# A fused attention, MLP and gated-convolution kernel: forty-eight VectorE operations moved to other engines, more buffers in the last stage, new planner numbers, issue in emission order

## The chip, the cores and the metric

The kernel runs on one core of one Trainium2 chip. The metric is the device time in microseconds (us) of one execution. The engines are PE (TensorE; PEld is its weight load), DVE (VectorE), ACT (ScalarE), POOL (GpSimd) and SP (SyncE, which here only issues DMAs).

## The reference

Three stages in a row, on 4 batches of 768 positions and 384 = 8 x 48 features, all in fp32:

```python
f = 1.0 / (1.0 + np.exp(-f_logit))
for t in range(S):                                   # gated linear attention, 8 heads of 48
    state = f[:, :, t, :, None] * state + np.einsum('bhd,bhe->bhde', k[:, :, t], v[:, :, t])
    y[:, :, t] = np.einsum('bhd,bhde->bhe', q[:, :, t], state)
...
xn = (x - mu) / np.sqrt(var + 1e-06) * g_ln          # layer norm, MLP 384 -> 1536 -> 384
ch = np.maximum(xn @ w_ch1, 0.0) @ w_ch2
x = x + ch
...
h = np.maximum(x @ w_in, 0.0)                        # 384 -> 1024, 3-tap convolution, gate
gate = 1.0 / (1.0 + np.exp(-conv_out))               # conv_out: 3 taps along the sequence
return (h * gate @ w_out).astype(np.float32)
```

## The kernel before, in words

The sequence is cut into 24 chunks `t` of 128 positions (6 per batch) and 8 units `u` of three chunks.

- `chunk(t)` is the attention of a chunk and the layer norm behind it. DVE scans the forget gate (`e`, L471) and its clipped inverse (`w`, L473), multiplies q by `e` (`qe`, L477), k by `w` (`kw`, L479), corrects that by one Newton step (L481, L483: the corrected k is what the scores wait for), and masks the scores (`am`, L502). Then come the sum `x` (ACT), its statistics (L640, L641), the reciprocal deviation `rs` on POOL (L645, L649), the normalized `xn` (DVE, L653), its fp16 high part (ACT) and low part (`xl`, DVE, L657), and a DMA transpose into `xnT`.
- `first(u)` and `second(u, tt)` are the MLP in pairs of fp16 numbers, three matmuls for each product. "c1" is its first half (L675 to L677), done chunk by chunk for the first two units and a unit at a time (384 columns) from the third on. "c2" is its second half (L744 to L746); behind it DVE adds the residual (`x2`, L756) and splits the sum (L761), and a DMA transposes it into `x2T`.
- `gate(u)` is the gated convolution: matmuls "h2" (L795 to L797), relu into `hr`, three taps into `cv` (L812, L817), the gate (L827, L832), and matmuls "o" (L846 to L848), then `ob` (ACT) and the output DMA.
- Weights arrive as raw 64-bit words; DVE decodes them (L374, L377, L380) and splits them (L421) in the first 140 us, between the work of the chunks.

What sets the order is `Plan`: each piece of work is a job with an engine, an assumed duration, a due time (`key`), what it depends on and which buffers it takes. `Plan.run` plays the jobs through in assumed time and emits their instructions in that order; the framework's own scheduler then reorders them once more for each engine. Due times come from a period `CP` per chunk and offsets (`T0`, `C1`, `C2`, `H2`, `O`, `EV`, `W1`, `W2`, `WI`). Each engine runs its instructions strictly in the order that results. All ACT instructions carry the line of the helper `act` (L316); they are told apart by tiles. Buffers: `hr`, `cv` two each, `ob` one, `x` five.

Of the kernel before, what the change touches and what calls it, by code (L numbers as in the profile page):

```python
# [20 lines left out]
DM = H * D  # L21
# [9 lines left out]
UT = 3  # L31
# [24 lines left out]
KV_DMA = 12  # L56
SW = CH + 1


CP = 22.8  # L60
T0 = 32.5
ATT = 0.3
C1 = 64.0
C2 = 21.0
H2 = 8.0
O = 39.0
EV = 29.0
# [8 lines left out]
def decode(nc, dst, tmp, raw):  # L76
    hi = raw[:, :, 1]
    nc.vector.tensor_scalar(
        out=tmp, in0=hi, scalar1=3, scalar2=0x3FFFFFFF,
        op0=ALU.logical_shift_left, op1=ALU.bitwise_and,  # L80
    )
    nc.vector.scalar_tensor_tensor(
        out=tmp, in0=hi, scalar=-0x40000000, in1=tmp, op0=ALU.bitwise_and, op1=ALU.bitwise_or
    )
    nc.vector.scalar_tensor_tensor(
        out=dst.bitcast(U32), in0=raw.bitcast(U32)[:, :, 0], scalar=29, in1=tmp.bitcast(U32),
        op0=ALU.logical_shift_right, op1=ALU.bitwise_or,
    )

# [24 lines left out]
class Plan:  # L114
# [7 lines left out]
    LAT = {"PE": 0.25, "DVE": 0.1, "ACT": 0.1, "POOL": 0.15, "SP": 2.5, None: 0.0}  # L122
# [37 lines left out]
    def run(self):  # L160
# [6 lines left out]
        while todo:  # L167
# [19 lines left out]
            free[e] = t + j.dur  # L187
            end = t + j.dur + j.lat
# [17 lines left out]
def fast_path(  # L206
# [20 lines left out]
    nc.vector.memset(fbs[0], 20.0)  # L227
# [6 lines left out]
    make_identity(nc, ident)  # L234
    d1 = const.tile([128, NP, SW], BF16, name="d1")
# [11 lines left out]
    nc.gpsimd.memset(fbs[1], 20.0)  # L247
# [32 lines left out]
    bufs("rs", 2, [128, 1], F32)  # L280
    bufs("xs", 2, [128, 2, DM], F16)
# [106 lines left out]
    def prep1(m, key):  # L388
# [10 lines left out]
        for z, kcs in enumerate(((0, 1), (2,))):  # L399
# [9 lines left out]
            j = P.job("PE", 0.55 * len(kcs), key, mm, [d, *his, J["diag"]], [bank], [use])  # L409
# [17 lines left out]
    def load_chunk(t):  # L427
        b, c = divmod(t, NCH)
        key = due_att(t) - 30.0

        def ldf():
            for j in range(2):
                nc.sync.dma_start(out=P("fb", t)[64 * j:64 * j + D, :, 1:], in_=f_[b, c, j])

        def ldqk():
            for j in range(2):
                nc.sync.dma_start(out=P("qk", t)[64 * j:64 * j + D], in_=qk_[b, c, j])

        def ldv():
            nc.sync.dma_start(out=P("vv", t), in_=v[b, c * CH:(c + 1) * CH, :])  # L440
        J["f", t] = transfer(0.9, key, ldf, ("fb", t), DM * CH * 4)
        J["qk", t] = transfer(0.9, key + 2.0, ldqk, ("qk", t), 2 * DM * CH * 4)
        J["v", t] = transfer(0.45, key + 4.0, ldv, ("vv", t), DM * CH * 4)

    def chunk(t):
# [19 lines left out]

        a1 = act(N, key + 1, e, fb, AF.Tanh, [J["f", t]], [E_], [F_], scale=0.5)
# [10 lines left out]
        qe = dv(N, 6, lambda: nc.vector.tensor_tensor(out=q_(), in0=q_(), in1=e3(), op=ALU.mult),  # L477
                [s1, J["qk", t]], (), [E_, Q_])
        kw = dv(N, 7, lambda: nc.vector.tensor_tensor(out=k_(), in0=k_(), in1=w3(), op=ALU.mult),  # L479
                [s2, J["qk", t]], (), [W_, Q_])  # L480
# [20 lines left out]
        sc = P.job("PE", 0.9, key + 10, scores, [kn, qe], [("sc", t)], [Q_])  # L501
# [15 lines left out]
        if not last and not dma:  # L517
# [15 lines left out]
            if c == 0:  # L533
# [6 lines left out]
                J["state", t] = P.job("DVE", 0.55, key + 14, upd, [kv], SN, [KV, E_])  # L540
            else:
# [10 lines left out]
                J["state", t] = P.job("DVE", 0.55, key + 14, upd, [j], SN, [K_, E_])  # L552
        elif not last:
# [10 lines left out]
                out=kT(), in_=ks().rearrange("p a b c -> p (a b c)")), [kl], [T_], [S_], lat=3.0)  # L564
# [8 lines left out]
            kv = P.job("PE", 0.65, key + 15, keyvals, [kT_, vl], [KV], [T_, ("vs", t)])  # L573
            if c == 0:
# [3 lines left out]
                J["state", t] = P.job("ACT", 0.5, key + 16, upd, [kv], SN, [KV])  # L578
            else:
# [11 lines left out]
                J["state", t] = P.job("DVE", 0.55, key + 16, upd, [j, kv], SN, [K_, KV])  # L591
# [3 lines left out]
        if c > 0:  # L595
# [6 lines left out]
            pre = [P.job("PE", 0.9, key + 16, inter, [qe, am, *old], [Y], [Q_, *SO])]  # L602
# [11 lines left out]
        else:  # L614
# [16 lines left out]
            ya = P.job("PE", 0.75, key + 17, intra, [al, vl, *pre], () if pre else [Y],  # L631
# [11 lines left out]
        def rstd():  # L643
# [6 lines left out]
        bn = P.job("DVE", 0.6, key + 19, stats, [xc], [ST], [X_])  # L650
        rs = P.job("POOL", 1.0, key + 20, rstd, [bn], [RS], [ST])
        N_, XS = ("xn", t), ("xs", t)
        xn = dv(DM, 21, lambda: nc.vector.tensor_scalar(  # L653
            out=P(*N_), in0=x(), scalar1=mv[:, 0:1], scalar2=P(*RS), op0=ALU.subtract,
            op1=ALU.mult), [rs], [N_], [X_, RS], V2)
        xh = act(DM, key + 22, lambda: P(*XS)[:, 0], lambda: P(*N_), AF.Copy, [xn], [XS], [N_])
        xl = dv(DM, 23, lambda: nc.vector.tensor_tensor(  # L657
            out=P(*XS)[:, 1], in0=P(*N_), in1=P(*XS)[:, 0], op=ALU.subtract), [xh], (), [N_, XS])
# [5 lines left out]
            [xl], () if tt else [XT], [XS] + ([XT] if tt else []), lat=3.0)  # L664
# [68 lines left out]
    def second(u, tt, started):  # L733
# [3 lines left out]
        bank = ("B", f"c2.{t}")  # L737
        o = lambda: P(*bank)[:, :DM]
        j = None
        for m0 in range(0, M1, 3):  # L740
            def mm(m0=m0):
                for m in range(m0, m0 + 3):
                    h = P(f"h{m}.{tt}", u)
                    nc.tensor.matmul(o(), h[:, 0], w2s[:, 0, m, :], start=(m == 0), stop=False)  # L744
# [4 lines left out]
                "PE", 1.47, key + 0.5 * m0, mm,  # L749
                [*(J["h", u, m, tt] for m in ms), *(z for m in ms for z in J["w2", m // 2]),  # L750
                 *([j] if j else started)],
                () if m0 else [bank], [(f"h{m}.{tt}", u) for m in ms] + ([bank] if m0 else []),
# [3 lines left out]
        x2 = P.job("DVE", V(DM), key, lambda: nc.vector.scalar_tensor_tensor(  # L756
            out=P(*X2), in0=o(), scalar=2.0 ** -9, in1=P("x", t), op0=ALU.mult, op1=ALU.add),
            [j], [X2], [bank, ("x", t)])
        h = act(DM, key, lambda: P(*XS)[:, 0], lambda: P(*X2), AF.Copy, [x2], [XS], [X2], scale=4.0)
        norm2(lambda: P(*X2), DM, X2_MAX ** -0.5, acc_col(), key + 1.0, [x2], [X2])  # L760
        lo = P.job("DVE", V(DM), key, lambda: nc.vector.scalar_tensor_tensor(  # L761
            out=P(*XS)[:, 1], in0=P(*X2), scalar=4.0, in1=P(*XS)[:, 0], op0=ALU.mult,
# [6 lines left out]
            lat=3.0)  # L769


    def gate(u):
# [9 lines left out]
        for m in range(M2):  # L782
# [38 lines left out]
            tp = P.job("DVE", 1.06, key, taps, [a], (), [HR, CV])  # L821
# [13 lines left out]
        for tt in range(UT):  # L835
# [18 lines left out]
            OB = ("ob", t)  # L854
# [53 lines left out]
    for u in range(NU):  # L908
        gate(u)
    for i, w_ in enumerate((w1s, w2s, wis, wos)):  # L910
# [5 lines left out]
    P.run()  # L916
# [270 lines left out]
```

## Time and profile before

| what | value |
|---|---|
| median of 3 runs (lowest, highest) | 645.26 us (643.96, 645.92) |
| the profiled execution: its own time / its span | 643.46 us / 641.4 us |
| busy PE, DVE, ACT, POOL | 586.1, 501.0, 386.2, 42.1 us (91, 78, 60, 7% of the span) |

The span runs from the first to the last instruction; 2.1 us of the profiled execution's own time lie outside it. Busy times are sums over the whole run: the early stretch, the middle and the end have different limits, so the shares say little until they are read stretch by stretch. On PE and DVE one instruction's shown duration reaches into the next one's, so that the distance between two starts is what an instruction costs in a queue without gaps.

### The profile page before, as it was taken

What the parts mean: (1) busy time and instruction counts of PE and PEld (TensorE: products, weight loads), DVE (VectorE), ACT (ScalarE), POOL (GpSimd) and SP (SyncE); (2) the same over time, 40 slices, a digit from 0 to 9 for tenths busy, and PEclk for the clock granted to TensorE, in tenths of its full rate; (3) what the DMA queues carried; (4) which work ended last, traced back from release to release, by engine and by line L of the source; (5) the groups of instructions that cost most, each with busy time, mean ns of one, the idle gap of its engine ahead of it and who ended that gap; (6) DMA issues with size and microseconds to landing.
All of it is one profiled execution on the core that took longest, in us unless ns stands there. A gap on an engine that the chain in (4) does not pass through costs nothing.

```text
span 641.4 us, 11836 instructions
## 1 busy us (share of the span) xinstructions
PE 586.1 (91%) x4680; PEld 392.7 (61%) x4680; DVE 501.0 (78%) x801; ACT 386.2 (60%) x798; POOL 42.1 (7%) x102
## 2 busy tenths in 40 slices
PE   1869898999798999999989999999989999999993
PEld 1758586767465666666656666666646666665551
DVE  6999989999999898976898787787895773326681
ACT  5888767779896575643675573554563662316471
POOL 3010110010101100010001000010000000000000
PEclk9979999999979899999989999999989999999998
DMA  8757567623224212541521203433221002001001
GB/s 255 184 168 186 175 141 181 189 55 75 68 58 123 63 41 48 143 77 28 103 54 54 80 20 75 118 78 58 46 42 50 14 13 51 25 1 38 25 13 42
DMA packets 75262, 52.24 MB, mean 81 GB/s; under 512 B 51904, under 2 KB 67264, under 8 KB 75200
## 3 DMA queue, kind: packets, MB, share of 16 engines
q1 hardware_dynamic: 75200, 51.42, 31.9%
q8 instruction: 38, 0.62, 0.4%
q14 instruction: 24, 0.20, 0.1%
HBM read 34.63 MB, written 4.72 MB: 61 GB/s over the span
## 4 chain that ended last, share of the span: by engine, by line
PE 53%; DVE 27%; ACT 8%; DMA 4%; issue 4%; POOL 2%; SPq 0%; DVEq 0%; ACTq 0%
PE B L675 5%; PE B L676 5%; PE B L677 5%; PE B L744 5%; PE B L746 5%; PE B L745 5%; PE B L848 4%; PE B L846 4%; PE B L847 4%; PE B L795 2%; PE B L796 2%; PE B L797 2%; DVE tw L377 2%; DVE cv L812 2%; DVE cv L827 2%
## 5 line engine op out<-in xcount | busy, mean ns | idle before, releaser
L675 PE MATMUL B<-xnT,w1s 128*128 128x128 f16 (+1 forms) x432 | 109.2, 275 | 3.0 <-DMA xnT<-xs 3.0
L677 PE MATMUL B<-xnT,w1s 128*128 128x128 f16 (+1 forms) x432 | 109.0, 275 | 0.3 <-ACT w1s L316 0.3
L676 PE MATMUL B<-xnT,w1s 128*128 128x128 f16 (+1 forms) x432 | 109.2, 275 | 0.0
L744 PE MATMUL B<-w2s,hh 128*128 128x384 f16 x288 | 94.5, 329 | 3.1 <-ACT w2s L316 2.1
L746 PE MATMUL B<-w2s,hh 128*128 128x384 f16 x288 | 94.7, 329 | 1.0 <-DVE hh L681 1.0
L745 PE MATMUL B<-w2s,hh 128*128 128x384 f16 x288 | 94.7, 329 | 0.9 <-DVE w2s L421 0.7
L681 DVE SCALAR_TENSOR_TENSOR hh<-B,hh 128x384 f16<-128x384 f32 (+1 forms) x90 | 51.4, 578 | 35.5 <-ACT hh L316 35.1
L795 PE MATMUL B<-x2T,wis 128*128 128x385 f16 x192 | 64.0, 334 | 5.9 <-ACT hr L316 5.9
L846 PE MATMUL B<-wos,g 128*128 128x384 f16 x192 | 63.7, 332 | 3.6 <-ACT g L316 3.6
L848 PE MATMUL B<-wos,g 128*128 128x384 f16 x192 | 63.3, 331 | 2.5 <-DVE g L832 2.4
L796 PE MATMUL B<-x2T,wis 128*128 128x385 f16 x192 | 64.1, 334 | 0.0
L797 PE MATMUL B<-x2T,wis 128*128 128x385 f16 x192 | 64.1, 334 | 0.0
L316 ACT ACTIVATE hh<-B 128x384 f16<-128x384 f32 (+1 forms) x90 | 44.5, 504 | 32.2 <-PE B L677 32.0
L847 PE MATMUL B<-wos,g 128*128 128x384 f16 x192 | 63.4, 330 | 0.0
L676 PEld LDWEIGHTS <-w1s 128*128 128x128 f16 x432 | 42.6, 99 | 16.8 <-issue 4.2
L675 PEld LDWEIGHTS <-w1s 128*128 128x128 f16 x432 | 43.3, 100 | 14.0 <-issue 0.7
L677 PEld LDWEIGHTS <-w1s 128*128 128x128 f16 x432 | 42.6, 99 | 14.9 <-issue 0.5
L812 DVE SCALAR_TENSOR_TENSOR cv<-hr,cws,cv 128x383 f32<-128x383 f32 (+1 forms) x64 | 38.8, 611 | 14.3 <-ACT cv L316 13.8
L497 PE MATMUL sc__144<-qk 64*128 64x128 f32 x384 | 29.6, 292 | 13.9 <-DVE qk L483 13.9
L746 PEld LDWEIGHTS <-hh 128*128 128x128 f16 x288 | 28.3, 98 | 21.8 <-issue 2.1
L744 PEld LDWEIGHTS <-hh 128*128 128x128 f16 x288 | 28.8, 100 | 20.6 <-issue 2.4
L316 ACT ACTIVATE cv<-hr,cws 128x384 f32<-128x384 f32 x64 | 38.7, 610 | 2.5 <-DVE g L832 1.3
(154 smaller groups left out, 1208.8 us busy)
## 6 DMA issues: line engine op xcount, KB each, us to landing
qk<-in_qk__dram SPq DMA_DIRECT2D x48, 192.0 KB, 3.5
raw<-in_w_dram SPq DMA_DIRECT2D x12, 768.0 KB, 5.4
vv<-in_v_dram SPq DMA_DIRECT2D x24, 192.0 KB, 2.5
fb<-in_f__dram SPq DMA_DIRECT2D x48, 96.0 KB, 2.7
out_dram<-ob SPq DMA_DIRECT2D x24, 192.0 KB, 1.9
raw<-in_wi_dram SPq DMA_DIRECT2D x6, 512.0 KB, 4.1
raw<-in_wo_dram SPq DMA_DIRECT2D x4, 768.0 KB, 4.3
xnT<-xs SPq DMA_TRANSPOSE x24, 2.5
```

Source lines behind the costliest of these rows:

```text
L316: nc.scalar.activation(out=out(), in_=in_(), func=func, **{a: z() if callable(z) else z for a, z in kw.items()},)
L675: nc.tensor.matmul(o, w1s[:, 0, kc, ms], x0, start=(kc == 0), stop=False)
L676: nc.tensor.matmul(o, w1s[:, 0, kc, ms], x1, start=False, stop=False)
L677: nc.tensor.matmul(o, w1s[:, 1, kc, ms], x0, start=False, stop=(kc == KC - 1))
L744: nc.tensor.matmul(o(), h[:, 0], w2s[:, 0, m, :], start=(m == 0), stop=False)
L745: nc.tensor.matmul(o(), h[:, 0], w2s[:, 1, m, :], start=False, stop=False)
L746: nc.tensor.matmul(o(), h[:, 1], w2s[:, 0, m, :], start=False, stop=(m == M1 - 1))
L796: nc.tensor.matmul(o, wis[:, 0, kc, ms], r1, start=False, stop=False)
L797: nc.tensor.matmul(o, wis[:, 1, kc, ms], r0, start=False, stop=(kc == KC - 1))
L846: nc.tensor.matmul(p, g[:, 0, ts_], wos[:, 0, m, :], start=(m == 0), stop=False)
L847: nc.tensor.matmul(p, g[:, 0, ts_], wos[:, 1, m, :], start=False, stop=False)
L848: nc.tensor.matmul(p, g[:, 1, ts_], wos[:, 0, m, :], start=False, stop=(m == M2 - 1))
```

## The change

- Chunks 0 to 9 (k: 1 to 9): the products `qe` and `kw` and the low part `xl` are computed by POOL. For these chunks ACT computes `xn` and its high part from `x` with a scale and a bias (a new POOL instruction makes the bias `mb`), in two independent passes.
- Chunks 0 to 8: the residual is added by PE: c2 begins with an fp32 matmul of `x` with a scaled identity (`ident2`), and ACT and DVE read the sum from PSUM. L756 goes for these chunks.
- The last stage gets more buffers: when the last two chunks are done with them, the two `qk` tiles become two more `hr`, and `am` and `as` two more `cv`; the output tiles of the last two units are taken from the five `x` tiles in place of the one `ob`.
- f is laid out by the host so that 128 partitions are filled by one DMA (before: two of 48 partitions each).
- The planner's assumed durations, latencies and due times have new numbers (one line of each kind is shown below), and `Plan.run` is called inside `tc.manual_schedule()`: what it emits is what each engine issues, in that order.

```diff
+POOL_Q = range(0, 10)
+POOL_K = range(1, 10)
+POOL_X = range(0, 10)
+XN_ACT = range(0, 10)
+X2_PE = range(0, 9)
+OBX = 2
...
-CP = 22.8
+CP = 22.6
...
-H2 = 8.0
+H2 = -23.6
...
+            if e == "POOL":
+                free["DVE"] += 0.2 * max(0.0, j.dur - 0.8)
...
+    G = lambda n: 0.15 + n * 2.2e-3
...
-            for j in range(2):
-                nc.sync.dma_start(out=P("fb", t)[64 * j:64 * j + D, :, 1:], in_=f_[b, c, j])
+            nc.sync.dma_start(out=P("fb", t)[:, :, 1:], in_=f_[b, c])
...
+        def tt(n, dk, fn, deps, takes=(), uses=(), pool=True):
+
+            if pool:
+                return P.job("POOL", G(n), key + dk, lambda: fn(nc.gpsimd), deps, takes, uses)
+            return dv(n, dk, lambda: fn(nc.vector), deps, takes, uses)
...
+        qe = tt(N, 6, lambda v_: v_.tensor_tensor(out=q_(), in0=q_(), in1=e3(), op=ALU.mult),
+                [s1, J["qk", t]], (), [E_, Q_], t in POOL_Q)
+        kw = tt(N, 7, lambda v_: v_.tensor_tensor(out=k_(), in0=k_(), in1=w3(), op=ALU.mult),
+                [s2, J["qk", t]], (), [W_, Q_], t in POOL_K)
...
+            scaled = lambda o, dk, deps, takes, uses: act(
+                DM, key + dk, o, x, AF.Identity, deps, takes, [*uses, X_, RS, MB],
+                scale=lambda: P(*RS), bias=lambda: P(*MB))
+            xn = scaled(lambda: P(*N_), 21, [mb], [N_], [])
+            xh = scaled(lambda: P(*XS)[:, 0], 22, [mb], [XS], [])
...
+        xl = tt(DM, 23, lambda v_: v_.tensor_tensor(
+            out=P(*XS)[:, 1], in0=P(*N_), in1=P(*XS)[:, 0], op=ALU.subtract), [xh], (), [N_, XS],
+            t in POOL_X)
...
+                if m0 == 0 and pe:
+                    nc.tensor.matmul(o(), ident2, P("x", t), start=True, stop=False)
...
+        if pe:
+            X2, x2, x2s_, two = bank, j, o, 2.0 ** -9
...
-            OB = ("ob", t)
+            OB = ("x", f"o{t}") if u >= NU - OBX else ("ob", t)
...
+    def more():
+
+        for name, a, shape in (
+            *(("hr", flat3(z), HT + 8) for z in qks),
+            ("cv", flat(P.pools["am"].tiles[0]), HT),
+            ("cv", flat3(P.pools["as"].tiles[0]).bitcast(F32), HT),
+        ):
...
-    P.run()
+    with tc.manual_schedule():
+        P.run()
```

How the queues move is shown at three places. First DVE at chunk 6, from its scan of `e` on, before the change; `tw`, `w__` and `wos` belong to the decoding of weights, `hh` to the MLP:

```order
L471 SCALAR_TENSOR_TENSOR e_111<-e_111,d_83 128x516
L756 SCALAR_TENSOR_TENSOR x_0_140<-B_148,x_127 128x384
L374 TENSOR_SCALAR tw_154<-raw_152 128x768
L477 TENSOR_TENSOR qk_70<-qk_70,e_111 128x512
L421 SCALAR_TENSOR_TENSOR wos<-w__0_155,wos 128x768
L761 SCALAR_TENSOR_TENSOR x2s_141<-x_0_140,x2s_141 128x384
L377 SCALAR_TENSOR_TENSOR tw_154<-raw_152,tw_154 128x768
L681 SCALAR_TENSOR_TENSOR hh_137<-B_150,hh_137 128x4x128
L380 SCALAR_TENSOR_TENSOR w__1_156<-raw_152,tw_154 128x768
L473 SCALAR_TENSOR_TENSOR w_113<-w_113,d_84 128x516
L502 SCALAR_TENSOR_TENSOR am_121<-sc__144,mask 128x1024
```

The same place of DVE's queue with the change (L499 is the scan of `e`, L501 that of `w`, L509 the Newton product, L811 the split behind c2):

```order
L499 SCALAR_TENSOR_TENSOR e_114<-e_114,d_85 128x516
L403 SCALAR_TENSOR_TENSOR w__1_160<-raw_157,tw_158 128x512
L397 TENSOR_SCALAR tw_158<-raw_155 128x768
L501 SCALAR_TENSOR_TENSOR w_115<-w_115,d_86 128x516
L444 SCALAR_TENSOR_TENSOR wis<-w__1_160,wis 128x512
L400 SCALAR_TENSOR_TENSOR tw_158<-raw_155,tw_158 128x768
L509 TENSOR_TENSOR w_115<-w_115,e_114 128x4x128
L403 SCALAR_TENSOR_TENSOR w__0_159<-raw_155,tw_158 128x768
L668 BN_STATS st_132<-x_126 128x6
L669 BN_AGGR mvs<-st_132 128x2
L811 SCALAR_TENSOR_TENSOR x2s_145<-B_149,x2s_145 128x384
```

The two products with q and k, the `x2` sum and `xn` are gone from the queue; the Newton product stands three rows behind the scan of `w` and now waits for POOL's product.

Second, POOL's queue around one chunk of the early stretch, before:

```order
L475 COPY pall<-e_111 128x4
L645 TENSOR_SCALAR rs_132<-mvs 128x1
L649 TENSOR_TENSOR rs_132<-rs_132,mhalf 128x1
L475 COPY pall<-e_112 128x4
L645 TENSOR_SCALAR rs_131<-mvs 128x1
L649 TENSOR_TENSOR rs_131<-rs_131,mhalf 128x1
```

and with the change:

```order
L505 TENSOR_TENSOR qk_71<-qk_71,e_114 128x512
L503 COPY pall<-e_114 128x4
L507 TENSOR_TENSOR qk_71<-qk_71,w_115 128x512
L673 TENSOR_SCALAR rs_133<-mvs 128x1
L677 TENSOR_TENSOR rs_133<-rs_133,mhalf 128x1
L683 TENSOR_SCALAR mb_135<-mvs,rs_133 128x1
L697 TENSOR_TENSOR xs_137<-xn_125,xs_137 128x384
```

Three products of 512 or 384 columns and the bias have come in; `rs` of one chunk now stands behind the products of another.

Third, PE at the first c2, with the change (before, L744 follows L677 there with nothing between):

```order
L718 MATMUL B_154<-xnT_139,w1s 128x128
L636 MATMUL B_150<-vv_116,am_123 128x48 x8
L785 MATMUL B_153<-x_126,ident_83 128x384
L788 LDWEIGHTS hh_141
L788 MATMUL B_153<-w2s,hh_141 128x384
```

The fp32 matmul L785 with the scaled identity (`ident2`, whose number the row leaves out) opens the accumulation of c2 in the same bank.

## Rows read from the trace of the kernel before

**Rows 1.** The page, 40 equal slices: busy tenths, granted TensorE clock in tenths.

```profile
PE   1869898999798999999989999999989999999993
PEclk9979999999979899999989999999989999999998
```

**Rows 2.** Stretches: us, each engine's busy us (instructions), PEclk, DMA share, GB/s.

```profile
0.00:16.00 16.00, 2.72 (x20) 2.50 (x21) 10.63 (x15) 8.17 (x19) 5.67 (x31) 1.00 0.85 255
16.00:219.00 203.00, 178.07 (x1709) 135.98 (x1708) 191.21 (x301) 160.14 (x355) 19.17 (x33) 0.95 0.50 130
...
320.00:360.00 40.00, 37.13 (x283) 23.59 (x282) 33.93 (x54) 24.06 (x45) 3.38 (x6) 0.96 0.23 62
...
440.00:480.00 40.00, 37.02 (x299) 23.91 (x298) 33.80 (x59) 23.67 (x48) 2.25 (x5) 0.96 0.30 53
480.00:595.00 115.00, 115.00 (x772) 70.92 (x769) 58.48 (x98) 50.08 (x96) 1.47 (x4) 1.00 0.10 27
595.00:633.00 38.00, 35.21 (x212) 19.96 (x210) 23.69 (x38) 20.74 (x35) 0.00 (x0) 1.00 0.06 21
```

**Rows 3.** Waits of PE, 13 to 219 us: total, times, longest.

```profile
PE sc__144 L497 <- DVE qk L483: 13.9, 3, 13.3
```

**Rows 4.** Waits of PE, 219 to 595 us.

```profile
PE B L795 <- ACT hr L316: 5.9, 2, 3.0
```

**Rows 5.** The end in order of time: last matmul of "o", last output copies.

```profile
631.96 0.33 PE L848 MATMUL B<-wos,g 128*128 128x384 f16 x1
...
634.35 0.49 ACT L316 ACTIVATE ob<-B 128x384 f32<-128x384 f32 x1 [1.99 <-DMA out_dram<-ob]
```

**Rows 6.** DVE in order of time at 120 us: start, duration in us.

```profile
119.71 0.56 DVE L756 SCALAR_TENSOR_TENSOR x<-B,x 128x384 f32<-128x384 f32 x1
120.18 0.55 DVE L374 TENSOR_SCALAR tw<-raw 128x768 int32<-128x768 int32 x1
120.65 0.68 DVE L477 TENSOR_TENSOR qk<-qk,e 128x512 f32<-128x512 f32 x1
121.25 0.95 DVE L421 SCALAR_TENSOR_TENSOR wos<-w__0_155,wos 128x768 f16<-128x768 f32 x1
```

**Rows 7.** Groups by line: shapes, count, busy us, mean ns of one, idle before.

```profile
L477 DVE TENSOR_TENSOR qk<-qk,e 128x512 f32<-128x512 f32 x24 | 16.4, 683 | 0.1
L756 DVE SCALAR_TENSOR_TENSOR x<-B,x 128x384 f32<-128x384 f32 x24 | 13.2, 551 | 23.4 <-PE B L746 23.2
...
L316 ACT ACTIVATE xs<-xn 128x384 f16<-128x384 f32 x24 | 12.5, 522 | 28.2 <-DVE xn L653 28.1
L653 DVE TENSOR_SCALAR xn<-x,mvs,rs 128x384 f32<-128x384 f32 x24 | 11.5, 479 | 15.2 <-POOL rs L649 15.2
```

**Rows 8.** The `x2` instructions of L756 alone, by stretches: us, DVE busy (instructions).

```profile
0.00:219.00 219.00, 3.31 (x6) 0.95 0.53 139
```

**Rows 9.** Waits of DVE, 16 to 219 us.

```profile
DVE xn L653 <- POOL rs L649: 5.8, 10, 0.7
```

**Rows 10.** POOL by shape: count, busy us, mean ns of one.

```profile
L248 POOL MEMSET qk<- 128x1024 f32 x1 | 1.0, 955 | 0.0
...
L924 POOL MEMSET one<- 128x1 f32 x1 | 0.1, 93 | 0.0
```

**Rows 11.** POOL's copy beside a DVE scan, and beside the masking that reads PSUM.

```profile
8.29 1.21 DVE L473 TENSOR_TENSOR_SCAN w<-w,d 128x516 f32<-128x516 f32 x1
...
8.43 1.04 POOL L475 COPY pall<-e 128x4 f32<-128x4 f32 x1 [3.58 <-DVE e L471]
...
17.73 1.20 DVE L502 SCALAR_TENSOR_TENSOR am<-sc__144,mask 128x1024 f32<-128x1024 f32 x1
17.87 0.19 POOL L475 COPY pall<-e 128x4 f32<-128x4 f32 x1 [7.97 <-DVE e L471]
```

**Rows 12.** PE in order of time at 22 us: an fp32 matmul of 256 columns.

```profile
22.29 0.60 PE L407 MATMUL B<-w__1_156,diag 128*128 128x256 f32 x2
22.72 0.27 PE L408 MATMUL B<-w1s,nident 128*128 128x256 f16 x1
```

More of the change, by code (lines that the diff above doesn't have):

```diff
@@ L121 @@
     ENGINES = ("PE", "DVE", "ACT", "POOL", "SP", "DMA", None)
-    LAT = {"PE": 0.25, "DVE": 0.1, "ACT": 0.1, "POOL": 0.15, "SP": 2.5, None: 0.0}
+    LAT = {"PE": 0.2, "DVE": 0.13, "ACT": 0.13, "POOL": 0.15, "SP": 2.5, None: 0.0}
     def __init__(self):
@@ L539, in upd @@
                         )
-                J["state", t] = P.job("DVE", 0.55, key + 14, upd, [kv], SN, [KV, E_])
+                J["state", t] = P.job("DVE", 0.75, key + 14, upd, [kv], SN, [KV, E_])
             else:
@@ L551, in upd @@
                         )
-                J["state", t] = P.job("DVE", 0.55, key + 14, upd, [j], SN, [K_, E_])
+                J["state", t] = P.job("DVE", 0.75, key + 14, upd, [j], SN, [K_, E_])
         elif not last:
@@ L590, in upd @@
                         )
-                J["state", t] = P.job("DVE", 0.55, key + 16, upd, [j, kv], SN, [K_, KV])
+                J["state", t] = P.job("DVE", 0.75, key + 16, upd, [j, kv], SN, [K_, KV])
         Y = ("B", f"y{t}")
@@ L741, in mm @@
             def mm(m0=m0):
+                if m0 == 0 and pe:
+                    nc.tensor.matmul(o(), ident2, P("x", t), start=True, stop=False)
                 for m in range(m0, m0 + 3):
                     h = P(f"h{m}.{tt}", u)
-                    nc.tensor.matmul(o(), h[:, 0], w2s[:, 0, m, :], start=(m == 0), stop=False)
+                    nc.tensor.matmul(
+                        o(), h[:, 0], w2s[:, 0, m, :], start=(m == 0 and not pe), stop=False)
                     nc.tensor.matmul(o(), h[:, 0], w2s[:, 1, m, :], start=False, stop=False)
@@ L748, in second @@
             j = P.job(
-                "PE", 1.47, key + 0.5 * m0, mm,
+                "PE", 1.47 + (0.66 if pe and not m0 else 0.0), key + 0.5 * m0, mm,
                 [*(J["h", u, m, tt] for m in ms), *(z for m in ms for z in J["w2", m // 2]),
                  *([j] if j else started)],
-                () if m0 else [bank], [(f"h{m}.{tt}", u) for m in ms] + ([bank] if m0 else []),
+                () if m0 else [bank],
+                [(f"h{m}.{tt}", u) for m in ms] + ([bank] if m0 else [("x", t)] if pe else []),
             )
@@ L755, in second @@
         X2, XS = ("x2", t), ("x2s", t)
[L756 to L760, printed above, removed]
+        if pe:
+            X2, x2, x2s_, two = bank, j, o, 2.0 ** -9
+        else:
+            x2s_, two = lambda: P(*X2), 1.0
+            x2 = P.job("DVE", V(DM), key, lambda: nc.vector.scalar_tensor_tensor(
+                out=P(*X2), in0=o(), scalar=2.0 ** -9, in1=P("x", t), op0=ALU.mult, op1=ALU.add),
+                [j], [X2], [bank, ("x", t)])
+        h = act(DM, key, lambda: P(*XS)[:, 0], x2s_, AF.Copy, [x2], [XS], [X2], scale=4.0 * two)
+        norm2(x2s_, DM, two * X2_MAX ** -0.5, acc_col(), key + 1.0, [x2], [X2])
         lo = P.job("DVE", V(DM), key, lambda: nc.vector.scalar_tensor_tensor(
[L762 removed]
+            out=P(*XS)[:, 1], in0=x2s_(), scalar=4.0 * two, in1=P(*XS)[:, 0], op0=ALU.mult,
             op1=ALU.subtract), [h], (), [X2, XS])
@@ L909, in fast_path @@
         gate(u)
+    def more():
[4 more added lines that the diff above has]
+        ):
+            s = P.pools[name]
+            s.free.append((mj.ready, len(s.tiles)))
+            s.tiles.append(a[:, :2 * shape].rearrange("p (a c) -> p a c", a=2))
+    mj = P.job(None, 0.0, 0.0, more, [J["late"], *(
+        j for j in P.jobs if any(
+            p in ("qk", "am", "as") and k in (NT - 2, NT - 1) for p, k in (*j.takes, *j.uses)))])
     for i, w_ in enumerate((w1s, w2s, wis, wos)):
```

91 lines of the change are left out of this document (52 added, 39 removed).

## The prediction

> **What bounds the kernel now.** I read the run by stretches, since the limits differ. The slices show PE nearly full from about 220 us to 600 us and full of holes before [rows 1]. [...] So three cases follow each other: a start of 13.3 us in which PE waits for the first corrected k [rows 3]; an early stretch to 219 us which DVE sets; and a PE-bound rest. In the rest only two holes of some 3 us show, in 320 to 360 and 440 to 480 us [rows 2], where PE waits for a relu on ACT to free a bank [rows 4]. At the end the last matmul starts at 631.96 us, but the last output copy only at 634.35 us, because it waited 1.99 us for the previous output DMA to free the one `ob` [rows 5].
>
> What the early stretch can give is bounded by PE: 203 - 178.07 = 24.9 us of idle time, and 203 x 0.05 = 10 us for the clock, 35 us together. Time saved on DVE later than 219 us is worth little.
>
> **What DVE loses in work.** An instruction of DVE costs the distance between starts: 120.18 - 119.71 = 0.47 us for one of 384 columns and 121.25 - 120.65 = 0.60 us for one of 512 [rows 6], each 0.08 us less than its mean duration of 551 or 683 ns; for `xn` that gives 479 - 80 = 0.40 us [rows 7]. Up to 219 us these go: ten `qe`, 6.0; nine `kw` (same shape), 5.4; ten `xl`, 4.7; ten `xn`, 4.0; and six of the nine `x2`, 2.8 (the other three fall into the PE-bound part [rows 8]). Besides, DVE waits ten times for POOL's `rs` ahead of `xn`, 5.8 us [rows 9]; with `xn` on ACT that wait leaves its queue. Sum: 28.7 us.
>
> **What POOL takes back.** POOL has 19 products of 512 columns and 10 of 384 to do, and no row shows one. A memset writes one stream: (955 - 93) / 1024 = 0.84 ns a column [rows 10]. A product that moves two streams at that rate, and has the 0.19 us of a small copy [rows 11] on top, takes 1.05 us for 512 columns and 0.84 for 384; one that moves three takes 1.48 and 1.16. I take the middle, 1.27 and 1.0: POOL is busy 34 us more (28 to 40). In the stretch it was busy 19.17 of 203 us [rows 2], so it has room.
>
> The price is what DVE loses meanwhile. The same copy took 1.04 us when it began beside a scan with two SBUF inputs, ending with it, and 0.19 us beside the masking, whose large input comes from PSUM [rows 11]. So a DVE instruction with two SBUF inputs keeps POOL from reading. Whether a long POOL instruction holds DVE up likewise no row shows, as POOL's were too short. The bounds are nothing and all of POOL's 40 us. I take half of the 34, 17 us: a product will often run beside DVE work that reads PSUM (masking, MLP low parts, state updates) or in a wait of DVE, but most of DVE's early work has two SBUF inputs (scans, decoding, splits). Net on DVE: -28.7 + 17 = -11.7 us, and PE follows, as it is DVE that releases it in this stretch.
>
> [...]
>
> **PE, ACT and the end.** An fp32 matmul of 256 columns holds PE for 22.72 - 22.29 = 0.43 us [rows 12], so one of 384 columns 0.65. Six of the nine residual matmuls lie in the early stretch, where PE's idle time covers them; without that cover they cost 3.9 us. Three lie in the PE-bound part: +2.0. ACT gets ten more passes of about 0.52 us [rows 7], 5 us on 160.14 busy of 203 [rows 2]: hidden while ACT is not the limit. Single f loads relieve SP's queue; I cost them at nothing, since only the first load is waited for. Behind the last matmul an `ob` from `x` no longer waits for the DMA: -1.9 (634.35 - 0.1 against 632.3). Extra `hr` and `cv` can close part of PE's idle time between 595 us and its end at 632.3: 37.3 - 35.2 = 2.1 us [rows 2, 5]; I take half, -1.0.
>
> **Order.** The planner's numbers and the fixed issue order move everything a little. In the PE-bound part the work is the same; the holes there, 5.9 us [rows 4], may close or others of that size open. I take zero, and 6 us either way in the range.
>
> Sum against the profiled execution's own time, 643.46 us: -11.7 + 2.0 - 1.9 - 1.0 = -12.6, so **631 us**. That execution lies 1.8 us under the median of the runs shown, so no correction is made.
>
> **Rivals.**
> - *POOL holds nothing up.* DVE gains all 28.7 us. PE has 35 us to give, so it can follow: 643.46 - 28.7 + 2.0 - 2.9 = 614 us, and 608 with the two holes closed. For it: DVE's reading of PSUM and its own waits leave POOL gaps. Against it: the POOL copies [rows 11] show that the two do share something. Chance 0.24.
> - *The lock in full (slower).* In the early DVE queue every POOL product stops DVE for its whole length. With 1.27 us each, 34 us come in for 28.7 that go; at the upper price 40. PE then finds no idle time for all nine residuals (+5.9): 643.46 + 5.3 + 5.9 - 1.9 = 653 us, 659 at the upper price. It decides once a POOL product blocks DVE on average for more than (28.7 + 0.9) / 29 = 1.02 us. For it: early on most of DVE's queue has two SBUF inputs, and three rows behind the scan of `w` DVE waits for the product anyway. Against: the masking and everything from PSUM passes. Chance 0.17.
> - *The chain, not the work.* `kw` is followed at once by the Newton product, and `xl` by the transpose, so POOL's slower pace, 0.67 and 0.5 us more, lies on the path of each early chunk; with two handovers it is some 1.2 us for each of ten chunks. If nothing else fills DVE's queue there, 12 us of the gain go and the time is 643 us: no change. Chance 0.09.
>
> The forecast (about half of POOL's time charged) has 0.50, with a range of its own of 622 to 640 us.
>
> **How the numbers follow.** The range is 612 to 647 us: it takes in the first rival nearly whole, the third, and the near part of the second; what it leaves out is the rest of the second (0.12) and of the first (0.06). A measurement of this kernel tells about 0.3% (2 us) from no change. Faster: the forecast, the first rival, and a little of the third, 0.75; within 0.3%: most of the third and edges, 0.08; slower 0.17.
>
> **What would show it.** Right: PE is full by about 200 us, not 219; DVE's busy time in the whole run is lower by 25 us or more; POOL's products last 1.0 to 1.5 us where DVE reads PSUM beside them; DVE's two-input instructions that start beside a POOL product are late or long by up to a microsecond; the last `ob` starts within 0.3 us of the last matmul. Wrong: products of 2 us or more on POOL, DVE waits for `qk` from POOL ahead of the Newton product in most early chunks, or new PE waits for more than 6 us between 219 and 600 us, which would be the order's doing.

## The result, and the profile after

The changed kernel took 625.13 us in the median of four runs (624.78 to 625.65); the kernel before took 644.61 us beside it (643.21 to 645.92). The ratio is 0.9699, with a 95% interval of 0.9675 to 0.9723: 3.0% faster, 19.5 us, of which 12.6 had been forecast. The profiled execution of after had a time of its own of 625.46 us and a span of 623.8 us; that of before 643.46 and 641.4.

The page of after, its 40 slices (to be held against [rows 1]); a slice is now 15.6 us:

```profile
PE   0889999899899999999999999999999999999994
DVE  4797999999998998599899995698996942315962
POOL 4451342423343100100000100010000000000000
PEclk9998999899999999999999999999999999999999
```

The holes of PE before 220 us are smaller, those behind it are gone up to 600 us, and the clock row shows 9 there throughout. The stretches, with each engine's busy us and count, the granted clock, the DMA share and GB/s, beside [rows 2]:

```profile
16.00:219.00 203.00, 189.18 (x1758) 146.41 (x1759) 190.13 (x263) 171.51 (x369) 67.99 (x68) 0.97 0.49 133
...
200.00:219.00 19.00, 19.00 (x129) 11.80 (x127) 18.74 (x31) 18.20 (x38) 3.25 (x4) 1.00 0.22 51
...
320.00:360.00 40.00, 40.00 (x305) 25.31 (x302) 38.55 (x62) 29.09 (x53) 4.17 (x6) 1.00 0.20 51
...
440.00:480.00 40.00, 40.00 (x287) 25.10 (x285) 35.22 (x59) 25.86 (x48) 0.74 (x2) 1.00 0.26 52
```

From 16 to 219 us PE is busy 11.1 us more; 3.9 of that are the six added residual matmuls, the rest is work brought forward (3.9 is an estimate, six times 0.65 us). DVE is busy as long as before (190.13 after 191.21) although 38 instructions fewer lie there. In both later stretches PE is full and the clock 1.00, where in before it was idle 2.9 and 3.0 us and the clock 0.96. The clock records of before and after show two levels, 1.00 and 0.50.

PE's waits over the whole run of after, with total, times and longest (three under 1 us in total are left out), to be held against [rows 3, 4]:

```profile
PE sc__148 L525 <- DVE qk L511: 15.9, 1, 15.9
PE sc__148 L525 <- issue: 5.2, 2, 3.1
PE B L557 <- ACT kts L336: 3.9, 3, 2.7
PE sc__148 L525 <- POOL rs L673: 2.0, 2, 1.5
PE B L716 <- DVE kts L570: 1.3, 1, 1.3
PE B L896 <- ACT g L336: 1.1, 1, 1.1
```

The wait for `hr` (5.9 us) is gone, and between 219 and 600 us no wait is left. In the early stretch a new one has come, which the names in these rows hide. All seven waits of the scores (L525) up to 219 us end 0.1 us after DVE's corrected k (L511) of that chunk, whatever the row names ("issue" is a wait for which the profile finds no releaser). So PE waits for the corrected k not once but seven times: 15.9 us at the start, 2.6 more than in [rows 3], and 8.6 us in six later places, where it was 0.6 us in before. The longest of the six, DVE, POOL and PE in order of time (start, duration):

```profile
40.67 1.69 DVE L576 TENSOR_TENSOR sb<-kts,e 48x192 f32<-48x192 f32 x2
...
43.27 1.41 DVE L509 TENSOR_TENSOR w<-w,e 128x512 f32<-128x512 f32 x1
...
46.06 0.68 DVE L511 SCALAR_TENSOR_TENSOR qk<-w,qk 128x512 f32<-128x512 f32 x1
...
40.29 1.49 POOL L507 TENSOR_TENSOR qk<-qk,w 128x512 f32<-128x512 f32 x1
42.58 1.55 POOL L697 TENSOR_TENSOR xs<-xn,xs 128x384 f16<-128x384 f32 x1 [0.80 <-ACT xs L336]
...
46.84 2.04 PE L525 MATMUL sc__148<-qk 64*128 64x128 f32 x15 [3.14 <-issue]
```

The first of the two instructions of L576 (1.32 us) and that of L509 (1.41) are 0.97 and 0.72 us longer than usual (0.35 and 0.68 us, the means in before), each beside a product of POOL. DVE has no gap from there to L511, so 1.7 of the 3.1 us are the products' doing. The granted clock is 0.50, the lower level, from 46.0 to 52.8 us.

At the end the last matmul starts at 617.14 us and the last output copy follows without a wait for a DMA (ACT in order of time; compare [rows 5]):

```profile
617.50 0.49 ACT L336 ACTIVATE x<-B 128x384 f32<-128x384 f32 x1 [1.46 <-PE B L898]
```

### The profile page after: what moved, and what is told of

Read it like the earlier page. It is cut to its first block, busy times and chain, and to the rows that moved or that the text cites. A ratio compares the mean times of both kernels' runs of the same rounds, so it can differ in the third digit from the quotient of the medians.

```text
span 623.8 us, 11788 instructions
## 1 busy us (share of the span) xinstructions
PE 586.1 (94%) x4698; PEld 398.0 (64%) x4698; DVE 495.9 (80%) x753; ACT 395.7 (63%) x808; POOL 95.4 (15%) x142
## 4 chain that ended last, share of the span: by engine, by line
PE 69%; DVE 21%; ACT 3%; DMA 2%; issue 2%; POOL 1%; SPq 0%; POOLq 0%
PE B L716 6%; PE B L717 6%; PE B L718 6%; PE B L788 6%; PE B L790 6%; PE B L791 6%; PE B L845 4%; PE B L847 4%; PE B L846 4%; PE B L898 4%; PE B L896 4%; PE B L897 4%; PE sc__148 L525 3%; DVE tw L400 2%; PE B L626 2%
## 5 line engine op out<-in xcount | busy, mean ns | idle before, releaser
L896 PE MATMUL B<-wos,g 128*128 128x384 f16 x192 | 62.6, 326 | 1.1 <-ACT g L336 1.1
L898 PE MATMUL B<-wos,g 128*128 128x384 f16 x192 | 62.6, 326 | 0.5 <-DVE vr L1009 0.5
L845 PE MATMUL B<-x2T,wis 128*128 128x385 f16 x192 | 62.9, 328 | 0.0
L847 PE MATMUL B<-x2T,wis 128*128 128x385 f16 x192 | 62.9, 327 | 0.0
L846 PE MATMUL B<-x2T,wis 128*128 128x385 f16 x192 | 62.9, 327 | 0.0
L897 PE MATMUL B<-wos,g 128*128 128x384 f16 x192 | 62.6, 326 | 0.0
L525 PE MATMUL sc__148<-qk 64*128 64x128 f32 x384 | 31.4, 308 | 24.5 <-DVE qk L511 15.9
L673 POOL TENSOR_SCALAR rs<-mvs 128x1 f32<-128x1 f32 x24 | 10.7, 444 | 243.3 <-DVE mvs L669 243.3
L525 PEld LDWEIGHTS sc__148<-qk 64*128 64x128 f32 x384 | 26.6, 209 | 31.1 <-issue 24.4
L862 DVE SCALAR_TENSOR_TENSOR cv<-hr,cws,cv 128x383 f32<-128x383 f32 (+1 forms) x56 | 35.8, 638 | 13.1 <-ACT cv L336 12.9
L788 PEld LDWEIGHTS <-hh 128*128 128x128 f16 x288 | 28.5, 99 | 18.7 <-ACT raw L372 0.3
```

The lines of the kernel that those rows point to most:

```text
L845: nc.tensor.matmul(o, wis[:, 0, kc, ms], r0, start=(kc == 0), stop=False)
L846: nc.tensor.matmul(o, wis[:, 0, kc, ms], r1, start=False, stop=False)
L847: nc.tensor.matmul(o, wis[:, 1, kc, ms], r0, start=False, stop=(kc == KC - 1))
L896: nc.tensor.matmul(p, g[:, 0, ts_], wos[:, 0, m, :], start=(m == 0), stop=False)
L897: nc.tensor.matmul(p, g[:, 0, ts_], wos[:, 1, m, :], start=False, stop=False)
L898: nc.tensor.matmul(p, g[:, 1, ts_], wos[:, 0, m, :], start=False, stop=(m == M2 - 1))
```

## What POOL's products cost

POOL's groups by line and shape in after (count, busy us, mean ns of one), which no row of before could show:

```profile
L505 POOL TENSOR_TENSOR qk<-qk,e 128x512 f32<-128x512 f32 x10 | 16.2, 1622 | 45.4 <-DVE e L499 29.5 <-PE B L430 14.0 <-PE B L550 1.8
L507 POOL TENSOR_TENSOR qk<-qk,w 128x512 f32<-128x512 f32 x9 | 13.6, 1508 | 18.2 <-DVE w L501 18.2
L697 POOL TENSOR_TENSOR xs<-xn,xs 128x384 f16<-128x384 f32 x10 | 13.1, 1315 | 11.6 <-ACT xs L336 11.6
```

These spans hold POOL's own waits for DVE, as two places show. The first is the `qe` of chunk 1, beside the masking; DVE and then POOL in order of time (start, duration):

```profile
18.07 1.22 DVE L530 SCALAR_TENSOR_TENSOR am<-sc__148,mask 128x1024 f32<-128x1024 f32 x1 [0.28 <-PE sc__148 L525]
...
17.93 1.18 POOL L505 TENSOR_TENSOR qk<-qk,e 128x512 f32<-128x512 f32 x1 [5.35 <-DVE e L499]
```

The second is a `qe` at 58 us, beside two DVE instructions whose inputs all lie in SBUF:

```profile
58.12 0.96 DVE L444 SCALAR_TENSOR_TENSOR w2s<-w__0_159,w2s 128x768 f16<-128x768 f32 x1
58.99 1.54 DVE L397 TENSOR_SCALAR tw<-raw 128x768 int32<-128x768 int32 x1
60.45 0.68 DVE L722 SCALAR_TENSOR_TENSOR hh<-B,hh 128x512 f16<-128x512 f32 x1
...
58.14 1.98 POOL L505 TENSOR_TENSOR qk<-qk,e 128x512 f32<-128x512 f32 x1 [14.01 <-PE B L430]
```

In the first place both run together at their undisturbed lengths: 1.22 us is the masking's, and 1.18 us is thus a product's. In the second the two take turns. DVE's split starts 0.02 us ahead of the product and keeps its 0.96 us; the product ends 60.12 - 59.08 = 1.04 us after it. DVE's next instruction, 0.55 us elsewhere, takes 1.54: it ends 0.41 us after the product. So each holds the other up for about what it has left; that it does so here is read from these two pairs, and the count below carries it over the run.

Over the whole run, each DVE instruction can be set against the median of its kind in the run without POOL's products (no_pool, below): 23 instructions of after are more than 0.1 us too long, 16.7 us in all, and every one of them runs beside a product. In no_pool not one is. Of the 27 that start inside a product with 0.3 us or more of it left, the 23 with all inputs in SBUF are all lengthened, and the four that read PSUM (two maskings, two `hh`) are not. That is the forecast's 17 us of blocking, and the two pairs above show it in both directions.

## The experiments

All kernels were timed against the kernel before in rounds on the same chip. "Ratio" is to that run of before (643.4 to 644.8 us), with its 95% interval; differences between kernels that were timed beside different runs of before are taken from the ratios, in per cent of 644.6 us; by the intervals each is uncertain by 2 to 6 us. The planner, or the framework's scheduler, orders each kernel's work anew, so what a piece is "worth" below includes the order that goes with it.

| kernel | median us | ratio | interval |
|---|---|---|---|
| after | 625.13 | 0.9699 | 0.9675 to 0.9723 |
| no_moves | 631.78 | 0.9817 | 0.9753 to 0.9880 |
| moves_only | 658.64 | 1.0244 | 1.0181 to 1.0307 |
| no_pool | 622.70 | 0.9694 | 0.9637 to 0.9751 |
| no_act_pe | 628.12 | 0.9773 | 0.9716 to 0.9829 |
| no_manual | 668.10 | 1.0346 | 1.0316 to 1.0376 |
| old_due | 634.32 | 0.9816 | 0.9784 to 0.9849 |
| before_manual | 652.27 | 1.0115 | 1.0095 to 1.0135 |
| no_buf | 629.89 | 0.9773 | 0.9747 to 0.9799 |
| best | 621.17 | 0.9645 | 0.9623 to 0.9668 |
| x_only | 621.09 | 0.9639 | 0.9613 to 0.9665 |
| dur_only | 636.06 | 0.9871 | 0.9846 to 0.9896 |
| no_moves_fw | 641.33 | 0.9948 | 0.9931 to 0.9964 |

**First question: which half of the change pays, the moves or the order?** My theory was that moves, order and end buffers each add a part (A); the rivals were that one of them carries all.

no_moves puts all 48 operations back on DVE:

```diff
-POOL_Q = range(0, 10)
-POOL_K = range(1, 10)
-POOL_X = range(0, 10)
-XN_ACT = range(0, 10)
-X2_PE = range(0, 9)
+POOL_Q = range(0)
+POOL_K = range(0)
+POOL_X = range(0)
+XN_ACT = range(0)
+X2_PE = range(0)
```

> All 48 operations are back on DVE; the new planner numbers, the fixed issue order, the f layout and the extra buffers stay. Theory A (two parts: DVE's early relief net of POOL's lock, and two holes closed by the schedule): the early part comes back, 7 us, and PE saves its 5.9 us of residual matmuls, of which 2 count; so about 630 us, with the holes at 330 and 470 us still closed. Rival B (all of the gain is schedule and buffers): 625 us or a little less. Rival C (all of it is the moved work): 640 us or more.

Measured 631.78 us, near theory A. Without a single move the kernel already gains 1.8%. PE is full from 320 to 360 us and from 440 to 480 us here too, so it is not the moves that close the two holes of [rows 2].

moves_only keeps the moves and gives up the rest:

```diff
-OBX = 2
+OBX = 0
-CP = 22.6
+CP = 22.8
...
-    with tc.manual_schedule():
-        P.run()
+    P.run()
```

(The other nine due-time numbers are those of before too, and `more()` adds no buffers.)

> The moved work and the f layout stay (with the planner's new durations); the due times are the old ones, the framework's scheduler orders the queues again, and the last stage has its old buffers. Theory A: PE is full by about 207 us as in the changed kernel, but the two holes of some 3 us with their clock dips (9 us) and the old end (4 us) are back: about 638 us. Rival B: 645 us. Rival C: 625 to 628 us.

Measured 658.64 us: 2.4% slower than before. All three expectations missed. The moves by themselves are a loss under the framework's scheduler, and something other than the sum of the parts is at work. PE waits 19.7 us, in eight waits, for `kts` on ACT, and DVE 7.0 us for POOL's `kw`.

no_pool and no_act_pe split the moves (first the three `POOL_` ranges emptied, then `XN_ACT` and `X2_PE`).

> The 29 products are back on DVE; xn on ACT, the residual on PE, and everything else as in the changed kernel. DVE gets back 10 x 0.60 + 9 x 0.60 + 10 x 0.47 = 16.1 us of work, and loses the 16.7 us by which its instructions were longer beside POOL's products in the changed kernel's trace. Theory A (lock as measured): the same within 3 us, 622 to 628. Rival D (products on POOL are nearly free for DVE, and the longer instructions sit in slack): 10 us or more slower, 635 or above.

Measured 622.70 us, theory A, with a ratio like that of after: POOL's 29 products bring nothing that shows (0.3 us slower with them than without, uncertain by some 4 us). What they cost PE is paid elsewhere without them: in no_pool it waits 3.2 us for the corrected k behind the first, not 8.6, and the granted clock is 1.00 there in every stretch up to 617 us (in after it is 0.50 for 10.2 us up to 219), but it waits 4.1 us for `xnT` and 3.0 for `hh`, of which after has neither.

> xn (ten) and the residual (nine) are back on DVE, the 29 products stay on POOL. DVE has 4.0 + 2.8 us more work and the wait for rs (5.8 us) in its queue up to the end of the early stretch, 12.6 us; PE has 5.9 us less. Theory A: early stretch 8 to 12 us longer, total 629 to 635. Rival B (schedule): 623 to 626.

Measured 628.12 us, between the two expectations; its interval overlaps those of after and of no_moves. Against no_moves, no_pool says the same thing from the other side: `xn` on ACT and the residual on PE are worth 1.2% (9.1 us by the two times, taken beside the same runs of before; 7.9 by the ratios).

**Second question: is it the fixed issue order, or the numbers?** Theory E: fixed order and refitted numbers belong together; F: the numbers alone do it; G: a fixed order helps only with the new numbers.

no_manual takes the fixed order out of after:

```diff
-    with tc.manual_schedule():
-        P.run()
+    P.run()
```

> The changed kernel with all its numbers, moves and buffers; only the framework's scheduler is let at the queues again. The moves under old due times and that scheduler came to 658 us. [...] Theory F (the old due times were at fault): 625 to 630 us.

Measured 668.10 us, far above theory F's range and 42 us above after by the ratios, with the same instructions. Its slices of PE and of the clock:

```profile
PE   2879897879787989999999899999997999999994
...
PEclk9879798979989799999999899999998999999998
```

The largest of PE's waits in the whole run, and of ACT's from 16 to 219 us:

```profile
PE B L557 <- ACT kts L336: 19.6, 4, 6.4
...
ACT xn L336 <- POOL mb L683: 20.4, 9, 3.4
ACT raw L372 <- DVE tw L400: 12.0, 7, 4.7
```

In after the first of these three was 3.9 us and that for `mb` 2.2, in three waits. The framework's scheduler puts `xn` into ACT's queue so early that it holds up what stands behind it, as here in order of time:

```profile
24.07 0.63 ACT L336 ACTIVATE e<-e 128x516 f32<-128x516 f32 x1
27.17 0.71 ACT L336 ACTIVATE xn<-x,mb,rs 128x384 f32<-128x384 f32 x1 [2.47 <-POOL mb L683]
27.78 0.69 ACT L336 ACTIVATE xs<-x,mb,rs 128x384 f16<-128x384 f32 x1
28.38 0.49 ACT L336 ACTIVATE w1s<-w__1_160,gl 128x256 f16<-128x256 f32 x1
```

`xn` and `w1s` stand still for 2.5 us behind a POOL instruction of one column, and PE, which multiplies with that `w1s` at 28.93 us (L431), waits 1.18 us for it.

old_due sets the due times of before into after (ten lines, drawn together here):

```diff
-CP = 22.6, CPL = 22.0, C1 = 63.0, C2 = 19.7, H2 = -23.6
-O = 46.1, EV = 38.7, W1 = 23.8, W2 = 52.3, WI = 95.7
+CP = 22.8, CPL = 22.8, C1 = 64.0, C2 = 21.0, H2 = 8.0
+O = 39.0, EV = 29.0, W1 = 20.0, W2 = 52.0, WI = 95.0
```

> The changed kernel with the ten due-time numbers of before; moves, buffers, planner durations and fixed issue order as changed. Theory F: 640 us or more, with new waits of PE in the middle or the end. Theory E: 625 to 632 us, since the order is still emitted as planned.

Measured 634.32 us: the ten numbers are worth 1.2% in after, between the two expectations. PE waits 7.6 us for the transposed `xnT` here.

before_manual adds the fixed order to the kernel before, and nothing else:

```diff
-    P.run()
+    with tc.manual_schedule():
+        P.run()
```

> The kernel before with one edit: each engine issues in the order of emission. Theory E, were it general: the scheduler's reordering costs something there too, 3 to 9 us faster than before (the two holes of 4.5 us each with their clock dips close). Theory G (a fixed order helps only with the newly fitted durations): the same as before or slower, 644 to 655 us.

Measured 652.27 us: 1.2% slower, in theory G's range. With the old assumed durations the order that the planner writes down is worse than what the scheduler makes of it. But not everywhere. From 219 to 595 us, in before and before_manual, and then in no_moves_fw and no_moves (below), which differ by the same switch:

```profile
219.00:595.00 376.00, 370.14 (x2745) 234.29 (x2743) 275.25 (x449) 196.70 (x389) 17.30 (x39) 0.99 0.24 54
...
219.00:595.00 376.00, 373.50 (x2803) 237.45 (x2802) 286.46 (x459) 203.73 (x399) 25.69 (x40) 1.00 0.24 56
...
219.00:595.00 376.00, 364.50 (x2721) 230.86 (x2720) 270.95 (x441) 188.81 (x376) 25.34 (x41) 0.99 0.26 59
...
219.00:595.00 376.00, 373.67 (x2818) 238.48 (x2816) 289.08 (x469) 202.50 (x397) 25.21 (x41) 1.00 0.26 59
```

The three pairs that differ by the switch alone, with PE's busy us and the granted clock in both stretches:

| framework's order -> fixed order | 16 to 219 us | 219 to 595 us |
|---|---|---|
| before -> before_manual | 178.1, 0.95 -> 174.5, 0.94 | 370.1, 0.99 -> 373.5, 1.00 |
| no_moves_fw -> no_moves | 182.2, 0.97 -> 180.6, 0.93 | 364.5, 0.99 -> 373.7, 1.00 |
| no_manual -> after | 169.6, 0.91 -> 189.2, 0.97 | 364.6, 0.98 -> 376.0, 1.00 |

In all three the fixed order itself closes most or all of the holes behind 219 us, with old numbers as with new. What decides whether it pays is the early stretch, where without moves it costs and with them it gives. In that of before_manual PE waits 14.6 us in five places for the corrected k behind the first, where it waited 0.6 us in before.

no_buf takes away the end buffers (`OBX = 0`, and `more()` adds none).

> The changed kernel with the old buffers at the end (one output tile, two hr, two cv). By the predicted terms: +1.9 us for the last output copy behind its DMA and up to +2.1 us for PE idle in the last 40 us, so 627 to 629 us. Rival: the planner fits the order to what buffers there are, and only the copy's 1.9 us show or nothing: 625 to 627 us.

Measured 629.89 us: they are worth 0.7%, 4.8 us, where 2.9 had been forecast; with 2 to 3 us of uncertainty the two are not clearly apart. The trace puts most of it in PE's waits for the gate: in the last 40 us before the last matmul ends PE is idle 4.3 us, 1.6 in after. The last copy starts 1.3 us after the last matmul has ended, where in before it was 2.1 and in after at once.

**Third question: what is left to separate, and what is best?**

dur_only is before_manual with the new assumed durations and latencies, the single f loads and the smaller first memsets (after without moves, with the due times of old_due and the buffers of no_buf).

> The kernel before with the fixed issue order, single f loads and the planner's new durations; due times, buffers and placement as before. With the fixed order alone it was 652.3 us; with durations, due times and buffers 631.8. Theory E (the due times are worth 9 us and the end buffers 4.6, as in the changed kernel): 644 to 648 us, the rest, 4 to 8 us, by durations. Theory F (an order that is fixed needs true durations above all): 634 to 640 us. Theory G (durations nothing, all by due times): 650 to 654 us.

Measured 636.06 us, in F's range: E had carried the due times' worth in after over to a kernel in which they are worth little. Under a fixed order the durations and the loads bring 2.4%, 16 us, and due times and end buffers together only 0.5% more, as long as nothing is moved (no_moves). This kernel changes the f loads and memsets along with the durations; how the 16 us divide was not tried.

no_moves_fw is no_moves without the fixed order.

> The change with all 48 operations back on DVE and without the fixed issue order (the framework's scheduler decides). With the fixed order it was 631.8 us. Theory E (the framework's scheduler loses against the planner's order whatever is moved): 640 to 655 us. Theory F (it loses 43 us only because work lies on POOL, ACT and PE that it does not place well): 629 to 637 us.

Measured 641.33 us, at E's lower edge: the scheduler loses 1.3% against the planner's order without moves and 6.5% with them (no_manual). So F is right on the larger part.

best and x_only are meant to be faster than after. best is no_pool with

```diff
-X2_PE = range(0, 9)
+X2_PE = range(0, 6)
```

> The change without POOL's 29 products, and with the residual on PE for the first six chunks only. Theory A (late residual matmuls cost PE time one for one, 0.65 us each, three of them; POOL's products are worth nothing): 622.7 less 2 us, 620 to 622 us. Theory B (the three late x2 back on DVE delay the low parts and open a wait on PE): 622.5 to 625 us.

x_only has `POOL_Q` and `POOL_K` empty and leaves the ten `xl` on POOL.

> The change with only the ten xl on POOL (qe and kw back on DVE). Theory A (each product on POOL takes from DVE about what it saves, whatever its width): as with no product on POOL, 621 to 624.5 us. Theory B (xl waits for ACT and comes where DVE reads PSUM, so that it saves its 4.7 us unpunished): 617 to 620.5 us.

Measured 621.17 and 621.09 us. Both lie in the range of their theory A, and both below after, by 0.5 and 0.6%, with intervals that don't meet its own: they beat both kernels. Whether either beats no_pool isn't settled, as its interval reaches over both; so what the three late residuals cost isn't shown by best. In x_only nine DVE instructions are lengthened, by 5.5 us, for ten products that save DVE 4.7: even the smaller product takes back what it gives. One of them, DVE and then POOL:

```profile
52.45 1.61 DVE L403 SCALAR_TENSOR_TENSOR w__0_159<-raw,tw 128x768 uint32<-128x768 uint32 x1
...
51.83 1.41 POOL L697 TENSOR_TENSOR xs<-xn,xs 128x384 f16<-128x384 f32 x1 [3.29 <-ACT xs L336]
```

The decode, 0.95 us when undisturbed, is 0.66 us longer.

## Why the prediction was right, and where it was off

The side was right, and so was the forecast case on POOL's price; the size was short by 7 us (of 19.5). Term by term, forecast against what the ratios give:

| term | forecast us | measured us | from |
|---|---|---|---|
| POOL's 29 products: saved, less blocking | -16.1 + 17 = +0.9 | +0.3 | after less no_pool |
| `xn`, `x2`, the wait for `rs`, late residual | -12.6 + 2.0 = -10.6 | -7.9 | no_pool less no_moves |
| end buffers | -2.9 | -4.8 | after less no_buf |
| order and planner's numbers | 0 | -7.0 | the rest of no_moves less before, when 4.8 of its 11.8 are the buffers' |

The last two rows depend on where the buffers are priced: without moves they were not tried alone, and there due times and buffers together bring only 3.5 us (dur_only against no_moves). Of the 11.8 us the fixed order alone gives 8.4 (no_moves against no_moves_fw).

**DVE beside POOL's products.** Half of POOL's time charged to DVE was a middle taken between bounds; it came out at the right size, 16.7 of 31.6 us, which is luck in part: nothing on record fixed the half. The forecast took 34 us of products; undisturbed they are 19 x 1.18 + 10 x 0.915 = 31.6 us (0.91 to 0.92 is what the three shortest of 384 columns took, and 1.18 the four shortest of 512), and the 42.9 us of the spans hold 11 us of waiting. DVE lost 16.7 us, 0.58 us a product, where 1.02 would have made the change a loss. The second rival, in which each product stops DVE for its whole length, did not come about since POOL as often was the one that waited (21 of the 29 products are over 0.1 us longer than undisturbed), and the first rival fell with the same rows.

**The chain.** DVE waits for a `kw` from POOL once, for 1.1 us, in the whole early stretch, not in most chunks. Other work filled its queue, as the forecast had it. But the corrected k came late all the same, in its turn behind lengthened instructions, and there it was PE that waited: 8.6 us in six places, 5.4 more than without the products (no_pool). So a part of the third rival's loss is there, on PE and not on DVE, and less than its 12 us. Under the framework's order DVE's wait for POOL's `kw` does appear: 5.6 us, four times, in no_manual.

**PE in the early stretch.** PE follows DVE, which in before was busy 191.21 of the 203 us from 16 to 219 beside PE's 178.07 at a clock of 0.95 [rows 2], but not fully. I set its work, by the usual distance between its starts for each kind, against the time (an estimate; the differences hold within 0.3 us whichever usual distance is taken, the totals do not, so only differences are given): at 219 us it had lost 10.9 us less in after than in before. 3.9 of that paid for the residual matmuls, so it was 7.0 us ahead, where 11.7 were expected. 2.6 us of the shortfall are the first k, which the forecast left where it was. ACT, DVE and POOL in after:

```profile
6.85 0.98 ACT L922 ACTIVATE diag<-ident,gl 128x128 f32<-128x128 f32 x3 [1.40 <-DVE gl L917]
...
7.94 0.62 ACT L336 ACTIVATE e<-e 128x516 f32<-128x516 f32 x1
...
11.05 1.48 DVE L507 TENSOR_TENSOR qk<-qk,w 128x512 f32<-128x512 f32 x1
...
9.98 2.01 POOL L505 TENSOR_TENSOR qk<-qk,e 128x512 f32<-128x512 f32 x1 [4.61 <-DVE e L499]
```

In the fixed order ACT makes `diag`, and waits for `gl`, ahead of its second pass over the first `e`. So that pass starts at 7.94 us and not at 6.41 as in before, though the first f came 1.1 us earlier (ACT's first pass over it starts at 4.20 us, in before at 5.26). That makes 1.5 us. In no_manual, with the same instructions, it starts at 5.46. The other 1.1 us arise behind it on DVE, although the 0.6 us of the `qe` have left its queue: that product, on POOL, lengthens DVE's `kw` of chunk 0 from 0.69 to 1.48 us, and DVE then waits 0.6 us for a weight. The 8.6 us of later waits for the corrected k lie in this stretch too.

**Order: the step that failed.** The prediction says of the holes that they "may close or others of that size open. I take zero, and 6 us either way in the range." By the same count PE lost 8.9 us less between 219 us and the tail in after than in before, more than the wait of [rows 4], because the clock dipped with each hole (to 0.50 for 3.4 us from 329.66 and from 469.61 us in before; by its mean, 0.04 of 80 us, 3.2 us more [rows 2]). No move closes them, since they are closed in no_moves, and no new number either: the fixed order alone leaves 2.5 of the 5.9 us and no dip of the clock there (before_manual). The choice of zero took the order for noise around a tuned state. The order is the largest lever in the change, in both directions: fixed, with the planner's old numbers, it costs 1.2% (before_manual); without it the kernel with the moves is 2.4% slower than before (moves_only) or, with the new due times and buffers, 3.5% (no_manual); with everything the change gives 3.0%.

**The end.** Span less the end of the last matmul fell from 9.1 us to 6.3, 2.8 less: 2.0 for the `ob` that no longer waits (1.9 forecast) and 0.8 behind the last copy. By the same count PE lost 1.1 us less in the tail (its idle time there fell from 2.2 to 1.6). Together with 7.0 and 8.9, less the late residual's 2.0, that is 17.8 us, and the span is 17.6 us shorter.

**The signs that I named.** The last copy follows the matmul at once; two-input DVE instructions are long by up to a microsecond beside a product; between 219 and 600 us no PE wait is left at all: so far all as said. One product of the 29, the first `qe`, lasted 2.01 us, which I had named as a sign of being wrong; with 1.18 us undisturbed, it is one that waited. PE is full from 200 us on (19.00 of 19 us to 219), as said. That DVE's busy time would fall by 25 us was wrong (501.0 to 495.9), for two reasons: lengthened instructions count as busy, and the sum depends on how many run back to back and overlap. It ranges from 499.6 us (no_moves_fw) to 511.1 (before_manual) for the same 801 instructions.

**What stays open.** Why moved work hurts so much under the framework's scheduler is shown by its waits (`xn` behind `mb`, 20.4 us on ACT; `kts`, 19.6 us on PE), but that these make up the 42 us is argued, not shown: no kernel had only `xn` set back under that scheduler. Where the time goes is on record: against after, PE in no_manual is idle 19.5 us more from 16 to 219 us and 11.4 more from 219 to 595, and its granted clock there is 0.91 and 0.98, where after has 0.97 and 1.00. That due times matter with the moves (1.2%) and hardly without (0.5%, buffers included) is measured, not explained. The same holds for the fixed order in the early stretch, which costs there without moves and gives with them.

## What to carry to other kernels

Before moving elementwise work from VectorE to GpSimd, count how much of VectorE's neighbouring work has all inputs in SBUF: each product here took back 0.58 us on average where it saved 0.47 to 0.60, so 29 moves came out at zero, while ten moves to ScalarE and nine to TensorE paid 1.2%. A fixed issue order is best tried together with measured durations behind it, not alone: the same switch was worth -1.2%, +1.3% and +6.5% in three settings. Read it stretch by stretch: it closed the late holes in all three and lost or won in the early stretch. When a change bundles an order with moves, do not price the order at zero because its work is unchanged; price the holes that it could close, with the clock lost behind them (here 5.9 us and 3.2 us). And when a list of waits names no releaser, or one that had long been done, look in order of time for what ended just before.

## What the runs showed of the hardware

- A VectorE instruction with a single SBUF input was held beside a GpSimd product too: the decode's first step (768 columns, 0.55 us undisturbed) took 1.54 us at 58.99 us.
- GpSimd's one-column `mb` stretched as well: it has a mean of 0.92 us in after, 0.26 at the least, and once, from 179.39 us, lasted 2.55 us and ended at 181.94, where a scan of VectorE ended at 181.96.
- In no_pool the granted clock is 1.00 from 16 to 219 us, where PE is busy 186.7 of the 203 us; in no_manual, with 169.6 us busy there, it is 0.91, and its row (above) shows 7 in four of the first fourteen slices. PE's two holes of [rows 2] cost more than their length: 5.9 us idle and, at a clock of 0.96 over 80 us, an estimated 3.2 us more.
